# Windowed attention into MoE on one core: short token blocks at both ends, loads ordered by need, wide rows for k as for q

## Chip, cores, metric

One NeuronCore of a Trainium2 chip. The metric is device time in microseconds, median of several executions; the profiled span is some 2 us shorter than the time of the same execution. A run is called slow when it is over 1.5% above the fastest of the same kernel. Ratios are the mean time of one kernel's fast runs over the mean of the other's fast runs of the same rounds, so they are not quite the ratio of the medians quoted.

## The reference, cut to what matters

```python
# q, k, v: (8 batches, 8 heads, 576 tokens, 64)
scores = q @ k.T / 8;  mask |i - j| <= 32;  attn = softmax(scores) @ v
x = attn, heads side by side              # 4608 tokens x 512
h = x @ w_in                              # 512 -> 2048
g = h if h >= 1, 0 if h <= -1, else (h + 1)**2 / 4
out = g @ w_out                           # 2048 -> 512, float32
```

## The kernel before: the parts that matter

"Group" m is four heads of a batch (two head pairs i); 16 groups. The kernel is one loop over steps. Every step issues, in a hand-written order, one 128-row slice of the MoE's first product (`hp`), a quarter of an output tile (`op`), and some attention events: transposes of q and k (`tpose`), three score groups per pair with exp and mask (`scores`), two half attentions per pair (`pv`). All loads cast fp32 to bf16 and are issued by GpSimd.

```python
def load_qk(m):        # q: 2 DMAs, rows of 9 tokens (2304 B); k: 4 DMAs, rows of one token (256 B)
    ...
def relay(m):          # q only: reorder on GpSimd so that the transposes get unit stride
    nc.gpsimd.tensor_copy(qj[m]..., qn[m]...)
def tpose(m, t):       # t 0,1: q -> qT on ScalarE;  t 2,3: k straight from PSUM into kz on VectorE
    ...
    else:
        for h in range(2):
            for g in range(2):
                nc.vector.tensor_copy(kz[2 * (m % 2) + g][r, j0:j1, h], ps[r, :n]...)
def scores(i, g):      # TensorE, exp on ScalarE, mask on GpSimd
    ...
    nc.gpsimd.tensor_mul(pt[i][:, seg], pt[i][:, seg], maskp[:, seg])
... # prologue: all of qk0, v0-3, qk1, masks, w_in, qk2, v4-7, w_out issued on GpSimd
for a in range(-1, OFF + 16 * (NBLK + 1)):     # 9 blocks of 512 tokens, 16 steps each
    ... # loads; hp (4 matmuls), Relu (ScalarE), max and min*mult (VectorE); scores; op (4 matmuls)
    if a in att_r: relay(att_r[a])             # one step before the group's first transpose
    if a in att_x: ... tpose(...) or pv(...)
```

`kz` holds k with zeros in the other head's half, so that two heads share one matmul. Below it is taken that each engine works through its queue in the order of the program.

The softmax here doesn't subtract the row's maximum and nothing guards it: scores larger than these inputs give would overflow.

## Time and profile before

| | before |
|---|---|
| time, three runs | 393.45 us (392.82 to 394.33) |
| first TensorE instruction | 39.37 us |
| first output matmul (`op`) | about 107.3 us |
| TensorE busy 107.2 to 376.9 us | 98.8% |
| GpSimd busy over the span | 219.9 us, 56% |

"Busy" is time in which an engine works on an instruction; the idle time in front of an instruction is put down to whatever released it. In the views PE is TensorE, PEld its weight loads, DVE VectorE, ACT ScalarE and POOL GpSimd; L165 is line 165 of that run's kernel; a bracket gives the idle time before an instruction and what ended it. TensorE is the bound from 107 us on, and the start is what can be won. The lines are in the prediction.

### The profile page before, as it was taken

Reading aid. Unit: us, or ns where it says so; the run is one execution under the profiler, and the core shown is the slowest. Engines: PE = TensorE matmul, PEld = TensorE weight load, DVE = VectorE, ACT = ScalarE, POOL = GpSimd, SP = SyncE. Lnnn points to the kernel's source line nnn. Section 1 sums busy time; section 2 is a strip of 40 time slices with the busy share of each in tenths; the row PEclk is TensorE's granted clock in tenths of the full one; section 3 lists DMA queues with packets and bytes.
Section 4 is the critical chain, followed back from the end, with each engine's and each line's share of the span. In section 5 each row is a group of like instructions: output and inputs, shape, how many; then the busy total and the mean of one; then the engine's idle time right before and its main releaser. Section 6 shows DMA issues by size and latency. Waiting matters only on the chain.

```text
span 391.7 us, 6070 instructions
## 1 busy us (share of the span) xinstructions
PE 322.4 (82%) x2136; PEld 177.9 (45%) x2176; DVE 289.0 (74%) x501; ACT 219.8 (56%) x469; POOL 219.9 (56%) x288
## 2 busy tenths in 40 slices
PE   0000765677699999999999999999999999999995
PEld 0000554444355555555555555555555544444442
DVE  6100332699899999999999999999998877787720
ACT  1000564666677767675867777776766644434421
POOL 8947889996776858694958768642422200000000
PEclk9999995899999999999999999999999999999999
DMA  9999996992939678794939395830000100101012
GB/s 81 99 195 141 172 163 47 73 78 18 77 26 120 77 71 93 67 96 51 104 42 104 45 128 65 83 43 27 28 28 28 54 28 27 54 28 52 29 55 80
DMA packets 88190, 28.18 MB, mean 72 GB/s; under 512 B 76896, under 2 KB 83040, under 8 KB 88160
## 3 DMA queue, kind: packets, MB, share of 16 engines
q0 software_dynamic: 82976, 18.36, 53.2%
q1 hardware_dynamic: 5184, 9.44, 6.4%
q8 instruction: 17, 0.28, 0.3%
q14 instruction: 13, 0.11, 0.1%
HBM read 36.70 MB, written 9.44 MB: 118 GB/s over the span
## 4 chain that ended last, share of the span: by engine, by line
PE 71%; POOL 11%; DVE 9%; DMA 3%; issue 2%; ACT 2%; another core or an unknown queue 1%; ACTq 0%; POOLq 0%
PE op L260 30%; PE hp L242 28%; DMA w_in<-in_moe_w_in_dram 3%; POOL vz L97 3%; PE nm L198 3%; DVE gT L249 3%; PE tp L149 3%; POOL pt L182 3%; PE sc L174 3%; DVE yy L248 3%; POOL kn L91 3%; PE dn L189 2%; PE dn L190 2%; DVE vz L106 1%; DVE xT L208 1%
## 5 line engine op out<-in xcount | busy, mean ns | idle before, releaser
L242 PE MATMUL hp<-xT,w_in 128*128 128x512 bf16 x555 | 146.0, 379 | 4.2 <-DVE xT L208 3.0
L260 PE MATMUL op<-w_out,gT 128*128 128x512 bf16 x557 | 142.3, 379 | 0.7
L249 DVE SCALAR_TENSOR_TENSOR gT<-rr,yy 128x512 bf16<-128x512 f32 x144 | 130.3, 905 | 5.1
L182 POOL TENSOR_TENSOR pt<-pt,maskp 128x352 bf16<-128x352 bf16 (+1 forms) x96 | 85.6, 907 | 79.2 <-ACT pt L181 78.8
L247 ACT ACTIVATE rr<-hp 128x512 f32<-128x512 f32 x144 | 86.1, 598 | 76.7 <-PE hp L242 71.6
L248 DVE TENSOR_TENSOR yy<-hp,rr 128x512 f32<-128x512 f32 x144 | 99.2, 689 | 26.7 <-ACT rr L247 24.4
L260 PEld LDWEIGHTS <-gT 128*128 128x128 bf16 x576 | 53.5, 98 | 51.7
L242 PEld LDWEIGHTS <-w_in 128*128 128x128 bf16 x576 | 51.9, 98 | 43.2 <-issue 0.2
L97 POOL DMA_DIRECT2D vz<-in_v_dram x64 | 48.7, 773 | 8.2 <-DMA w_in<-in_moe_w_in_dram 7.4
L160 DVE COPY kz<-tp 64x320 bf16<-64x320 bf16 (+1 forms) x128 | 33.2, 298 | 25.8 <-PE tp L149 25.3
L149 PE MATMUL tp<-ident,qj 128*128 128x128 bf16 x144 | 15.2, 242 | 44.6 <-POOL qj L137 43.8
L153 ACT COPY qT<-tp 128x320 bf16<-128x320 bf16 (+1 forms) x64 | 24.8, 454 | 47.9 <-PE tp L149 47.7
L91 POOL DMA_DIRECT2D kn<-in_k_dram x64 | 47.9, 791 | 0.9 <-PE tp L149 0.9
L181 ACT ACTIVATE pt<-sc 128x352 bf16<-128x352 f32 (+1 forms) x96 | 45.0, 468 | 2.0 <-PE sc L174 1.8
L208 DVE TENSOR_TENSOR xT<-nm,rc 128x288 bf16<-128x288 f32 x64 | 28.8, 449 | 16.8 <-ACT rc L204 16.8
L203 ACT ACTIVATE lr<-dn 128x288 f32<-128x288 f32 x64 | 26.5, 414 | 19.8 <-PE dn L190 19.8
L174 PEld LDWEIGHTS <-kz 128*128 128x128 bf16 x288 | 25.0, 104 | 25.6 <-issue 6.4
L149 PEld LDWEIGHTS <-qj 128*128 128x128 bf16 x144 | 10.6, 108 | 52.9 <-POOL qj L137 49.4
L174 PE MATMUL sc<-qT,kz 128*128 128x128 bf16 (+1 forms) x288 | 33.2, 228 | 1.6 <-ACT pt L181 1.2
L198 PE MATMUL nm<-pt,vz 128*128 128x128 bf16 (+2 forms) x320 | 27.7, 221 | 7.5 <-DVE xT L208 7.5
L264 ACT COPY osb<-op 128x512 f32<-128x512 f32 x36 | 21.1, 587 | 19.4 <-PE op L260 16.6
L198 PEld LDWEIGHTS <-vz 128*128 128x128 bf16 x320 | 22.2, 103 | 17.8 <-issue 12.5
(26 smaller groups left out, 158.8 us busy)
## 6 DMA issues: line engine op xcount, KB each, us to landing
out_dram<-osb SPq DMA_DIRECT2D x36, 256.0 KB, 2.0
qn<-in_q_dram POOLq DMA_DIRECT2D x32, 144.0 KB, 3.6
kn<-in_k_dram POOLq DMA_DIRECT2D x64, 72.0 KB, 4.4
vz<-in_v_dram POOLq DMA_DIRECT2D x64, 72.0 KB, 3.0
w_in<-in_moe_w_in_dram POOLq DMA_DIRECT2D x1, 2048.0 KB, 12.8
w_out<-in_moe_w_out_dram POOLq DMA_DIRECT2D x1, 2048.0 KB, 15.0
```

The source lines that it names most:

```text
L91: nc.gpsimd.dma_start(out=kn[m][64 * g:64 * g + 64, :, h], in_=k[b, 4 * qd + 2 * g + h].rearrange("(c p) d -> p c d", p=64))
L97: nc.gpsimd.dma_start(out=vz[i % 8][64 * h:64 * h + 64, :, 64 * h:64 * h + 64], in_=v[b, 2 * hp + h].rearrange("(c p) d -> p c d", p=64))
L149: nc.tensor.transpose(ps[:, j - j0], src[:, j].rearrange("p h d -> p (h d)"), ident)
L174: nc.tensor.matmul(ps[:, off:off + q1 - q0], kz[2 * (m % 2) + gg][:, c].rearrange("d h r -> d (h r)"), qT[m][:, gg, q0:q1], start=True, st ...
L181: nc.scalar.activation(pt[i][:, seg], ps[:, :off], AF.Exp, scale=D ** -0.5)
L182: nc.gpsimd.tensor_mul(pt[i][:, seg], pt[i][:, seg], maskp[:, seg])
L198: nc.tensor.matmul(nm[:, q0 - lo:q1 - lo], vz[i % 8][:, c], pt[i][:, pcol(c, q0):pcol(c, q1)], start=n == 0, stop=n == len(parts) - 1, ski ...
L242: nc.tensor.matmul(hp, w_in[:, kk, 128 * f:128 * f + 128], xT[:, kk, TB * blk:TB * blk + TB], start=kk == 0, stop=kk == 3)
L247: nc.scalar.activation(rr, hp, AF.Relu, scale=0.5, bias=0.5)
L248: nc.vector.tensor_max(yy, hp, rr)
L249: nc.vector.scalar_tensor_tensor(gT[blk][:, f], rr, 1.0, yy, op0=ALU.min, op1=ALU.mult)
L260: nc.tensor.matmul(op, gT[blk - 1][:, ff, 128 * tt:128 * tt + 128], w_out[:, ff], start=ff == 0, stop=ff == 15)
```

## The change

Its intent: start the MoE when 256 tokens of batch 0 are ready instead of 512 (blocks 256, 8 x 512, 256); load first what is needed first, weights in pieces; read k, like q, in rows of nine tokens with one DMA per group instead of four; let VectorE carry the first half batch's relays, masks and copies so that GpSimd can issue loads.

k in rows of nine tokens arrives interleaved. So it needs a relay as q does, and after the transpose a second copy, `zfill`, which puts it into the zero-padded `kz`. In the main loop relays and zfill are on GpSimd.

```diff
+            rows = src[b, 4 * qd:4 * qd + 4].rearrange("(h g) s d -> h (g s) d", g=2)
+            nc.gpsimd.dma_start(out=t, in_=rows.rearrange("h (x j) d -> x h (j d)", j=NC))   # q and k
...
+    load_qk(0); identity; load_qk(1); masks; v0, v1 (five of nine chunks); w_in[:512]; rest of v0, v1; (abridged)
+    load_qk(2); w_in[512:]; v2; load_qk(3); v3; w_out in four pieces                             (abridged)
...
-            for h in range(2):
-                for g in range(2):
-                    nc.vector.tensor_copy(kz[2 * (m % 2) + g][r, j0:j1, h], ...)
+            nc.vector.tensor_copy(o, i)          # k -> kT, as q -> qT
+    def zfill(m, g, eng):
+        for h in range(2):
+            eng.tensor_copy(kz[2 * (m % 2) + g][r, :, h], kT[m][r, g]...)
...
+    # prologue: half of batch 0, relays, zfill and masks on VectorE
+    sizes = [256] + [512] * 8 + [256]
...
+            at(a0 - 10 + 2 * t + (3 if early else 0), "t", 2 * b, t)      # transposes
+            at(a0 + t if early else a0 - 2 + 2 * t, "t", 2 * b + 1, t)
...
+                rel.setdefault(a - 1, []).append((e[1], e[2] // 2))       # relay: a step before
+                zf.setdefault(a, []).append(e[1])                         # zfill: after the last transpose of k
```

Two score groups of a pair now take 352 and 256 columns, the third 480.

More of the change, by code (lines that the diff above doesn't have):

```diff
@@ L37, with pc @@
     HALF = S // 2
-    TB = 512
-    NBLK = NT // TB
     def qrange(c):
         return max(0, 64 * c - 32), min(S, 64 * c + 96)
-    def pcol(c, qq):
-        return qq if c % 2 == 0 else S + qq - 32
-    PW = 2 * S - 64
-    GROUPS = [(0, 2, 4), (6, 8, 1), (3, 5, 7)]
+    GROUPS = [(0, 2, 4), (1, 3), (6, 8, 5, 7)]
+    pcol, PW = {}, 0
+    for c in (1, 3, 0, 2, 4, 6, 8, 5, 7):
+        pcol[c] = PW
+        PW += qrange(c)[1] - qrange(c)[0]
+    def pc(c, qq):
+        return pcol[c] + qq - qrange(c)[0]
     const = ctx.enter_context(tc.tile_pool(name="const", bufs=1))
@@ L54 @@
     qtp = ctx.enter_context(tc.tile_pool(name="qtp", bufs=2))
-    ptp = ctx.enter_context(tc.tile_pool(name="ptp", bufs=3))
+    ptp = ctx.enter_context(tc.tile_pool(name="ptp", bufs=4))
     smp = ctx.enter_context(tc.tile_pool(name="smp", bufs=2))
@@ L73, with load_qk @@
     kz = [const.tile([128, NC, 2, 64], BF, name=f"kz{i}") for i in range(4)]
-    vz = [const.tile([128, NC, 128], BF, name=f"vz{i}") for i in range(8)]
+    vz = [const.tile([128, 2, NC, 128], BF, name=f"vz{i}") for i in range(4)]
     ctx.enter_context(tc.manual_schedule())
     qn, kn = {}, {}
-    def load_qk(m):
+    def load_qk(m, which="qk"):
         b, qd = divmod(m, 2)
-        qn[m] = qkn.tile([128, 2, S], BF, name="qn")
-        kn[m] = qkn.tile([128, NC, 2, D], BF, name="kn")
-        for g in range(2):
-            h0 = 4 * qd + 2 * g
-            nc.gpsimd.dma_start(out=qn[m][64 * g:64 * g + 64],
-                                in_=q[b, h0:h0 + 2].rearrange("h (p j) d -> p h (j d)", j=NC))
-        for g in range(2):
-            for h in range(2):
-                nc.gpsimd.dma_start(out=kn[m][64 * g:64 * g + 64, :, h],
-                                    in_=k[b, 4 * qd + 2 * g + h].rearrange("(c p) d -> p c d", p=64))
@@ L94, in load_v @@
-    def load_v(i):
-        b, hp = divmod(i, H // 2)
-        for h in range(2):
-            nc.gpsimd.dma_start(
-                out=vz[i % 8][64 * h:64 * h + 64, :, 64 * h:64 * h + 64],
-                in_=v[b, 2 * hp + h].rearrange("(c p) d -> p c d", p=64))
+        for src, dst, nm in ((q, qn, "qn"), (k, kn, "kn")):
+            if nm[0] in which:
+                t = dst[m] = qkn.tile([128, 2, S], BF, name=nm)
+                rows = src[b, 4 * qd:4 * qd + 4].rearrange("(h g) s d -> h (g s) d", g=2)
+                nc.gpsimd.dma_start(out=t, in_=rows.rearrange("h (x j) d -> x h (j d)", j=NC))
@@ new lines, in load_v @@
+    def load_v(m, c0=0, c1=NC):
+        b, qd = divmod(m, 2)
+        for h in range(2):
+            h0 = 4 * qd + 2 * h
+            o = vz[m % 4][64 * h:64 * h + 64, :, :, 64 * h:64 * h + 64]
+            i = v[b, h0:h0 + 2].rearrange("g s d -> (g s) d").rearrange("(gc r) d -> r gc d", r=64)
+            if c0 == 0 and c1 == NC:
+                nc.gpsimd.dma_start(out=o.rearrange("r g c d -> r (g c) d"), in_=i)
+            else:
+                for g in range(2):
+                    nc.gpsimd.dma_start(out=o[:, g, c0:c1], in_=i[:, NC * g + c0:NC * g + c1])
@@ new lines, in load_w_in, with load_w_out @@
+    def load_w_in(f0, f1):
+        src = moe_w_in.rearrange("(qd h g d) f -> h qd d g f", qd=2, h=2, g=2)
+        for h in range(2):
+            for qd in range(2):
+                nc.gpsimd.dma_start(out=w_in[64 * h:64 * h + 64, 2 * qd:2 * qd + 2, f0:f1],
+                                    in_=src[h, qd, :, :, f0:f1])
+    def load_w_out(n):
+        nc.gpsimd.dma_start(out=w_out[:, 4 * n:4 * n + 4],
+                            in_=moe_w_out.rearrange("(ko ki) f -> ki ko f", ki=128)[:, 4 * n:4 * n + 4])
@@ L101, with zero @@
     nc.scalar.preload_act_table_set("natural_log_exp_and_others")
     load_qk(0)
-    for t in kz:
-        nc.vector.memset(t.rearrange("p c h r -> p (c h r)").bitcast(FP), 0.0)
-    for i in range(8):
-        nc.vector.memset(vz[i].rearrange("p c d -> p (c d)").bitcast(FP), 0.0)
-    make_identity(nc, ident)
-    for i in range(4):
-        load_v(i)
-    load_qk(1)
+    make_identity(nc, ident)
+    load_qk(1)
+    def zero(t):
+        for h in range(2):
+            if len(t.shape) == 4 and t.shape[2] == 2:
+                z = t[64 * h:64 * h + 64, :, 1 - h]
+            else:
+                z = t[64 * h:64 * h + 64, :, :, 64 * (1 - h):64 * (1 - h) + 64].rearrange("r g c d -> r (g c) d")
+            nc.vector.memset(z, 0.0)
@@ L112 @@
+    for t in kz:
+        zero(t)
+    for t in vz:
+        zero(t)
     nc.gpsimd.memset(mask1, 1.0)
@@ L115 @@
         r = slice(64 * h, 64 * h + 64)
-        nc.gpsimd.memset(ones2[r, r], 1.0)
         nc.gpsimd.affine_select(out=mask1[r], in_=mask1[r], compare_op=ALU.is_ge, fill=0.0, base=0,
@@ L120 @@
                                 channel_multiplier=1, pattern=[[-1, 128]])
+        nc.gpsimd.memset(ones2[r, r], 1.0)
+    load_v(0, 0, 5)
+    load_v(1, 0, 5)
     for c in range(NC):
@@ L123 @@
         j0 = q0 - (64 * c - 32)
-        nc.vector.tensor_copy(maskp[:, pcol(c, q0):pcol(c, q0) + q1 - q0], mask1[:, j0:j0 + q1 - q0])
-    nc.gpsimd.dma_start(out=w_in, in_=moe_w_in.rearrange("(ko ki) f -> ki ko f", ki=128))
+        nc.vector.tensor_copy(maskp[:, pcol[c]:pcol[c] + q1 - q0], mask1[:, j0:j0 + q1 - q0])
+    load_w_in(0, 512)
+    load_v(0, 5, NC)
+    load_v(1, 5, NC)
     load_qk(2)
-    for i in range(4, 8):
-        load_v(i)
-    nc.gpsimd.dma_start(out=w_out, in_=moe_w_out.rearrange("(ko ki) f -> ki ko f", ki=128))
@@ L132, with relay @@
-    qj, qT = {}, {}
-    def relay(m):
-        qj[m] = qjp.tile([128, NC, 2, D], BF, name="qj")
-        nc.gpsimd.tensor_copy(qj[m].rearrange("p j h d -> p h j d"),
-                              qn[m].rearrange("p h (j d) -> p h j d", d=D))
+    load_w_in(512, DFF)
+    load_v(2)
+    load_qk(3)
+    load_v(3)
+    for n in range(4):
+        load_w_out(n)
+    qj, kj, qT, kT = {}, {}, {}, {}
+    def relay(m, t, eng):
+        src, dst, nm = ((qn, qj, "qj"), (kn, kj, "kj"))[t]
+        dst[m] = qjp.tile([128, NC, 2, D], BF, name=nm)
+        eng.tensor_copy(dst[m].rearrange("p j h d -> p h j d"),
+                        src[m].rearrange("p h (j d) -> p h j d", d=D))
@@ L140 @@
     TJ = [(0, 5), (5, 9)]
     def tpose(m, t):
-        src, (j0, j1) = (qj if t < 2 else kn)[m], TJ[t % 2]
+        src, dst = ((qj, qT), (kj, kT))[t // 2]
+        j0, j1 = TJ[t % 2]
+        if t % 2 == 0:
+            dst[m] = qtp.tile([128, 2, S], BF, name="qT" if t < 2 else "kT")
         ps = ps_s.tile([128, 5, 128], BF, name="tp", tag="sc")
-        if t == 0:
-            qT[m] = qtp.tile([128, 2, S], BF, name="qT")
         for j in range(j0, j1):
-            nc.tensor.transpose(ps[:, j - j0], src[:, j].rearrange("p h d -> p (h d)"), ident)
@@ L150, in tpose @@
-        n = j1 - j0
+            nc.tensor.transpose(ps[:, j - j0], src[m][:, j].rearrange("p h d -> p (h d)"), ident)
+        o = dst[m].rearrange("d g (p j) -> d g p j", j=NC)[:, :, :, j0:j1]
+        i = ps[:, :j1 - j0].rearrange("d j (g p) -> d g p j", g=2)
         if t < 2:
-            for g in range(2):
-                nc.scalar.copy(
-                    qT[m][:, g].rearrange("d (p j) -> d p j", j=NC)[:, :, j0:j1],
-                    ps[:, :n].rearrange("d j (g p) -> d g p j", g=2)[:, g])
-        else:
-            for h in range(2):
-                for g in range(2):
-                    r = slice(64 * h, 64 * h + 64)
-                    nc.vector.tensor_copy(kz[2 * (m % 2) + g][r, j0:j1, h],
-                                          ps[r, :n].rearrange("d c (g p) -> d g c p", g=2)[:, g])
+            nc.scalar.copy(o, i)
+        else:
+            nc.vector.tensor_copy(o, i)
@@ L163, with scores @@
+    def zfill(m, g, eng):
+        for h in range(2):
+            r = slice(64 * h, 64 * h + 64)
+            eng.tensor_copy(kz[2 * (m % 2) + g][r, :, h], kT[m][r, g].rearrange("d (c r) -> d c r", r=64))
     pt = {}
-    def scores(i, g):
+    def scores(i, g, eng):
         m, gg = divmod(i, 2)
@@ L170, in scores @@
         off = 0
-        first = None
         for c in GROUPS[g]:
@@ L175, in scores @@
                              qT[m][:, gg, q0:q1], start=True, stop=True)
-            if first is None:
-                first = pcol(c, q0)
             off += q1 - q0
-        seg = slice(first, first + off)
+        seg = slice(pcol[GROUPS[g][0]], pcol[GROUPS[g][0]] + off)
         nc.scalar.activation(pt[i][:, seg], ps[:, :off], AF.Exp, scale=D ** -0.5)
-        nc.gpsimd.tensor_mul(pt[i][:, seg], pt[i][:, seg], maskp[:, seg])
+        eng.tensor_mul(pt[i][:, seg], pt[i][:, seg], maskp[:, seg])
     def pv(i, hf):
@@ L187, in pv @@
         nm = ps_n.tile([128, HALF], FP, name="nm")
-        o0, o1 = max(lo, 32), min(hi, S - 32)
-        nc.tensor.matmul(dn, ones2, pt[i][:, lo:hi], start=True, stop=False)
-        nc.tensor.matmul(dn[:, o0 - lo:o1 - lo], ones2, pt[i][:, pcol(1, o0):pcol(1, o1)], start=False, stop=True)
+        odd = (1, 3) if hf == 0 else (5, 7)
+        e0 = pc(2 * hf * 2, lo) if hf else pc(0, 0)
+        o0, o1 = qrange(odd[0])[0], qrange(odd[1])[1]
+        nc.tensor.matmul(dn, ones2, pt[i][:, e0:e0 + HALF], start=True, stop=False)
+        nc.tensor.matmul(dn[:, o0 - lo:o1 - lo], ones2, pt[i][:, pcol[odd[0]]:pcol[odd[0]] + o1 - o0],
+                         start=False, stop=True)
         parts = []
@@ L197, in pv @@
         for n, (c, q0, q1) in enumerate(parts):
-            nc.tensor.matmul(nm[:, q0 - lo:q1 - lo], vz[i % 8][:, c], pt[i][:, pcol(c, q0):pcol(c, q1)],
+            nc.tensor.matmul(nm[:, q0 - lo:q1 - lo], vz[i // 2 % 4][:, i % 2, c], pt[i][:, pc(c, q0):pc(c, q0) + q1 - q0],
                              start=n == 0, stop=n == len(parts) - 1, skip_group_check=True)
@@ L208, in mul @@
             nc.vector.tensor_mul(xT[:, hp, b * S + lo:b * S + hi], nm, rc)
-        return mul
-    A0 = 9
-    att_s, att_x, att_r = {}, {}, {}
-    for m in range(NP // 2):
-        for t in range(4):
-            att_x[8 * m + 2 * t] = ("t", m, t)
-        att_r[8 * m - 1] = m
-    for i in range(NP):
-        for g in range(3):
-            att_s[A0 + 4 * i + g] = (i, g)
-        for hf in range(2):
-            att_x[A0 + 4 * i + 4 + 2 * hf] = ("v", i, hf)
-    OFF = A0 + 4 * 3 + 6 + 2
-    loads = {}
@@ L225, with flush @@
-    for m in range(3, NP // 2):
-        loads.setdefault(8 * m - 16, []).append((load_qk, m))
-    for i in range(8, NP):
-        loads.setdefault(4 * i - 14, []).append((load_v, i))
-    gT = {}
-    mul = None
-    for a in range(-1, OFF + 16 * (NBLK + 1)):
-        mm = a - OFF
-        blk, f = divmod(mm, 16)
-        for fn, arg in loads.get(a, []):
-            fn(arg)
-        if 0 <= mm and blk < NBLK:
+        muls.append(mul)
+    muls = []
+    def flush():
+        while muls:
+            muls.pop(0)()
@@ new lines @@
+    V, P = nc.vector, nc.gpsimd
+    for m in range(2):
+        for t in range(2):
+            relay(m, t, V)
+    for m in range(2):
+        if m == 1:
+            for i in range(2):
+                for g in range(2):
+                    scores(i, g, V)
+        for t in range(4):
+            tpose(m, t)
+        for g in range(2):
+            zfill(m, g, V)
+        if m == 1:
+            for i in range(2):
+                pv(i, 0)
+                flush()
+    for i in range(2, 4):
+        for g in range(2):
+            scores(i, g, V)
@@ new lines, with at @@
+    for i in range(2, 4):
+        pv(i, 0)
+        flush()
+    sizes = [256] + [512] * 8 + [256]
+    starts = [sum(sizes[:t]) for t in range(len(sizes))]
+    NB = len(sizes)
+    ev = {}
+    def at(a, *e):
+        ev.setdefault(a, []).append(e)
+    for i in range(4):
+        at(i, "s", i, 2)
+        at(i + 1, "v", i, 1)
+    for t in range(4):
+        at(t, "t", 2, t)
+        at(4 + t, "t", 3, t)
+    for n in range(12):
+        at(4 + n, "s", 4 + n // 3, n % 3)
+    for n in range(4):
+        at(4 + 3 * n + 2, "v", 4 + n, 0)
+        at(4 + 3 * n + 3, "v", 4 + n, 1)
@@ new lines @@
+    for b in range(2, B):
+        a0 = 16 * (b - 1)
+        early = b == 2
+        for n in range(4):
+            for g in range(3):
+                at(a0 + 4 * n + g - (0 if early and n == 0 else 2), "s", 4 * b + n, g)
+            at(a0 + 4 * n + 1 + (1 if early and n == 0 else 0), "v", 4 * b + n, 0)
+            at(a0 + 4 * n + 3, "v", 4 * b + n, 1)
+        for t in range(4):
+            at(a0 - 10 + 2 * t + (3 if early else 0), "t", 2 * b, t)
+            at(a0 + t if early else a0 - 2 + 2 * t, "t", 2 * b + 1, t)
@@ new lines @@
+    rel, zf = {}, {}
+    for a, es in ev.items():
+        for e in es:
+            if e[0] == "t" and e[2] % 2 == 0:
+                rel.setdefault(a - 1, []).append((e[1], e[2] // 2))
+            if e[0] == "t" and e[2] == 3:
+                zf.setdefault(a, []).append(e[1])
+    loads = {}
+    for m in range(4, NP // 2):
+        loads.setdefault(max(0, 8 * m - 38), []).append((load_qk, m))
+        loads.setdefault({4: 3, 5: 5, 6: 11, 7: 17}.get(m, 8 * m - 39), []).append((load_v, m))
@@ L238 @@
+    for e in rel.get(-1, []):
+        relay(*e, P)
+    gT = {}
+    for a in range(16 * NB + 8):
+        t, f = divmod(a, 16)
+        for fn, m in loads.get(a, []):
+            fn(m)
+        if t < NB:
+            n, t0 = sizes[t], starts[t]
             if f == 0:
-                gT[blk] = gtp.tile([128, 16, TB], BF, name="gT")
-            hp = ps_h.tile([128, TB], FP, name="hp")
+                flush()
+                gT[t] = gtp.tile([128, 16, 512], BF, name="gT")
+            hp = ps_h.tile([128, 512], FP, name="hp")
@@ L241 @@
             for kk in range(4):
-                nc.tensor.matmul(hp, w_in[:, kk, 128 * f:128 * f + 128], xT[:, kk, TB * blk:TB * blk + TB],
+                nc.tensor.matmul(hp[:, :n], w_in[:, kk, 128 * f:128 * f + 128], xT[:, kk, t0:t0 + n],
                                  start=kk == 0, stop=kk == 3)
-            rr = ewp.tile([128, TB], FP, name="rr")
-            yy = ewp.tile([128, TB], FP, name="yy")
-            nc.scalar.activation(rr, hp, AF.Relu, scale=0.5, bias=0.5)
-            nc.vector.tensor_max(yy, hp, rr)
@@ L249 @@
-            nc.vector.scalar_tensor_tensor(gT[blk][:, f], rr, 1.0, yy, op0=ALU.min, op1=ALU.mult)
-        if mul:
-            mul()
-            mul = None
-        if a in att_s:
-            scores(*att_s[a])
-        if 1 <= blk <= NBLK and mm >= 0:
-            tt, f0 = divmod(f, 4)
-            if f0 == 0:
-                op = ps_o.tile([128, DM], FP, name="op")
-            for ff in range(4 * f0, 4 * f0 + 4):
-                nc.tensor.matmul(op, gT[blk - 1][:, ff, 128 * tt:128 * tt + 128], w_out[:, ff],
-                                 start=ff == 0, stop=ff == 15)
-            if f0 == 3:
-                osb = osp.tile([128, DM], FP, name="osb")
-                nc.scalar.copy(osb, op)
-                t0 = TB * (blk - 1) + 128 * tt
-                nc.sync.dma_start(out=out[t0:t0 + 128, :], in_=osb)
@@ L267 @@
-        if a in att_r:
-            relay(att_r[a])
-        if a in att_x:
-            kind, i, t = att_x[a]
-            if kind == "t":
-                tpose(i, t)
-            else:
-                mul = pv(i, t)
+            rr = ewp.tile([128, 512], FP, name="rr")
+            yy = ewp.tile([128, 512], FP, name="yy")
+            nc.scalar.activation(rr[:, :n], hp[:, :n], AF.Relu, scale=0.5, bias=0.5)
+            nc.vector.tensor_max(yy[:, :n], hp[:, :n], rr[:, :n])
+            nc.vector.scalar_tensor_tensor(gT[t][:, f, :n], rr[:, :n], 1.0, yy[:, :n], op0=ALU.min, op1=ALU.mult)
@@ new lines @@
+        flush()
+        es = ev.get(a, [])
+        for e in es:
+            if e[0] == "s":
+                scores(e[1], e[2], P)
+        if t >= 1:
+            per = sizes[t - 1] // 128 if t < NB else 4
+            for x in range(per * f, per * f + per):
+                tt, ff = divmod(x, 16)
+                if ff == 0:
+                    op = ps_o.tile([128, DM], FP, name="op")
+                nc.tensor.matmul(op, gT[t - 1][:, ff, 128 * tt:128 * tt + 128], w_out[:, ff],
+                                 start=ff == 0, stop=ff == 15)
+                if ff == 15:
+                    osb = osp.tile([128, DM], FP, name="osb")
+                    nc.scalar.copy(osb, op)
+                    r0 = starts[t - 1] + 128 * tt
+                    nc.sync.dma_start(out=out[r0:r0 + 128, :], in_=osb)
@@ L278 @@
+        for e in rel.get(a, []):
+            relay(*e, P)
+        for e in es:
+            if e[0] == "t":
+                tpose(e[1], e[2])
+        for m in zf.get(a, []):
+            for g in range(2):
+                zfill(m, g, P)
+        for e in es:
+            if e[0] == "v":
+                pv(e[1], e[2])
 _INS = ['q', 'k', 'v', 'moe_w_in', 'moe_w_out']
```

## The prediction

> **What bounds the kernel now.** I read the page's slices first, then the table of busy time by stage, the groups, the GpSimd and TensorE timelines of the start, and the issue table.
>
> The slices (40 of 9.8 us each) show where TensorE is idle:
>
> ```profile
> PE   0000765677699999999999999999999999999995
> POOL 8947889996776858694958768642422200000000
> DMA  9999996992939678794939395830000100101012
> DMA packets 88190, 28.18 MB, mean 72 GB/s; under 512 B 76896, under 2 KB 83040, under 8 KB 88160
> ```
>
> TensorE is empty for four slices, half busy for seven, and full from slice 11 to the end. GpSimd and DMA are full while TensorE is not. The stages (columns: stretch, length, busy us of PE, PEld, DVE, ACT, POOL, clock, DMA share, GB/s) put numbers on it:
>
> ```profile
> 0.00:39.37 39.37, 0.00 (x0) 0.00 (x1) 7.79 (x21) 1.28 (x1) 29.94 (x52) 1.00 1.26 128
> 39.37:71.00 31.63, 21.16 (x169) 16.88 (x171) 9.22 (x31) 18.32 (x47) 29.55 (x39) 0.84 1.15 129
> 71.00:107.20 36.20, 24.07 (x192) 13.73 (x195) 32.18 (x59) 22.72 (x53) 31.24 (x39) 1.00 0.74 57
> 107.20:376.90 269.70, 266.43 (x1728) 142.48 (x1762) 239.86 (x391) 175.19 (x365) 129.13 (x161) 1.00 0.44 59
> ```
>
> Nothing runs on TensorE before 39.37 us. From there to 71 us the attention prologue is paced by GpSimd (29.55 of 31.63 us busy); from 71 to 107.2 us the first MoE block runs with both GpSimd and VectorE near 88%. From 107.2 us, the first output matmul, TensorE is 98.8% busy and sets the pace. So all there is to win lies before 107 us. The GpSimd timeline says why the first transpose waits until 39.37 us:
>
> ```profile
> 18.23 0.78 POOL L125 DMA_DIRECT2D w_in<-in_moe_w_in_dram  x1
> ...
> 31.36 0.73 POOL L97 DMA_DIRECT2D vz<-in_v_dram  x1 [7.42 <-DMA w_in<-in_moe_w_in_dram]
> ...
> 36.92 1.21 POOL L129 DMA_DIRECT2D w_out<-in_moe_w_out_dram  x1
> 38.18 2.23 POOL L137 COPY qj<-qn 128x1152 bf16<-128x1152 bf16 x2
> ```
>
> The relay copy of q, which feeds the first transpose, stands on GpSimd behind all the load issues, and one of these waits 7.42 us for w_in to land. The instruction list shows the reason: the GpSimd loads use eight completion semaphores in turn, so load n waits for load n-8. The groups give the unit costs that I use below:
>
> ```profile
> L249 DVE SCALAR_TENSOR_TENSOR gT<-rr,yy 128x512 bf16<-128x512 f32 x144 | 130.3, 905 | 5.1
> L182 POOL TENSOR_TENSOR pt<-pt,maskp 128x352 bf16<-128x352 bf16 x64 | 56.6, 886 | 59.8 <-ACT pt L181 59.5
> L182 POOL TENSOR_TENSOR pt<-pt,maskp 128x384 bf16<-128x384 bf16 x32 | 30.4, 949 | 19.4 <-ACT pt L181 19.2
> L137 POOL COPY qj<-qn 128x1152 bf16<-128x1152 bf16 x16 | 18.2, 1144 | 0.0
> ```
>
> **What the Trainium skill says.** "DMA: Bandwidth & Descriptors", section Specifications, asks for at least 512 B per descriptor for line rate. The trace agrees in kind: 76,896 of 88,190 packets are under 512 B, and the DMA moves 81 to 99 GB/s (bytes written) in the first two slices, which hold q, k and v, against 195 in the slice that holds w_in. "VectorE: DVE Perf Modes", section The perf-mode tier table, gives bf16 SBUF copies four elements per cycle on VectorE and bf16 tensor_tensor two. No such large operation runs on VectorE in the kernel before, so the prologue's times on VectorE below are estimates from that page. "SBUF — State Buffer" says that a VectorE instruction with two SBUF inputs contends with a GpSimd instruction that reads SBUF. The trace agrees: L249 has a minimum of 691 ns, a mean of 905 ns, and 692 ns after 320 us, where GpSimd is idle.
>
> **The change, part by part.**
>
> *Loads.* k goes from 64 DMAs of 256-byte reads (mean 791 ns of GpSimd each) to 16, q from 32 to 16, each of 256 packets. From the issue costs of the present 128, 576 and 2048-packet loads (634, 773, 1214 ns: about 0.3 ns a packet) a q or k load costs 0.67 us, a whole v load (1152 packets, 32 of them if none were split) 0.94 us. Over the kernel GpSimd issue falls from 117 to about 60 us. But that is spread out, and most of it lies beside a full TensorE.
>
> *Relay, zero filling and masks.* k now needs a relay too (16 x 1.14 us), and the copies into kz (zfill) become GpSimd work after the first two groups: 56 copies of 64x576, estimated at half a relay plus overhead, 0.63 us. In the first half batch all this is on VectorE, with the masks. VectorE's kz copies (8 per group, 298 ns, 2.4 us) become two wide ones, about 0.75 us each.
>
> *The prologue.* GpSimd's first four loads are issued by about 4.7 us. q and k, 0.59 MB of fp32 each, need about 1.6 us at the 380 GB/s read rate that w_in shows (4.2 MB from about 19.6 to 31 us), so group 0 lands near 6.5 and group 1 near 10 us. VectorE clears kz and vz until about 8 us, copies masks (1.34 us as now) and relays. First transpose about 10 us instead of 39.4. Then follow transpose, evacuate, zfill, four scores with exp and mask, group 1, and four half attentions in series, each about 2 us for Ln, Exp and multiply: the prologue would end near 28 to 30 us.
>
> *The new wait.* After-order on GpSimd: all loads through the fourth piece of w_out are issued before the first relay of group 2. By the rule of eight, that last piece is issued only when the second half of v group 2 has landed. Up to there DMA must bring six q/k loads (9.5 us at 380 GB/s), three groups of v (2304 packets each; 9216 small packets of k and v took about 13.5 us in the first stage now, so 3.3 us a group, 10 us) and w_in (11 us): 30.5 us, plus 2.8 us start, about 1.5 us of starving on issue and 2 us landing: about 37 us. GpSimd is free at 38.4 us, hardly earlier than the 38.18 us of today. TensorE meets the transpose of group 2 in step 0 of the MoE, so it stands from about 29 until 39.6 us. **Much of the prologue's gain is thus given back.**
>
> *Block 0 (256 tokens).* Until block 1 can start, GpSimd has six relays (6.9), four masks of 480 columns left from batch 0 (slope 2 ns a column from the two rows above: 1.14 each, 4.6), the twelve masks of batch 1 (0.886 + 0.70 + 1.14 per pair, 10.9), eight zfills (5.0), six q/k loads (4.0) and six v loads (5.6): 37.0 us. About 2 us more go to v4 waiting for the lanes that w_out holds, and 2 us to bubbles (GpSimd was 93% busy in the comparable stage). TensorE has only 64 x 0.108 = 6.9 us of MoE and 10 us of attention here, VectorE about 26 us. So GpSimd binds, and block 1 starts at 38.4 + 41 + 1, **about 80 us**.
>
> *From there to the end.* A matmul of 512 columns takes 0.216 us (17 in 3.67 us at 373.14 us in the chain). The 269.7 us from 107.2 us hold 8 x 128 of them, 221.1 us; the other 48.6 us are the 22.9 head pairs of attention that I count as left then, 2.12 us each, 8.5 us a batch. After: block 1 has 96 matmuls and one batch, 29.2 us on TensorE, but VectorE needs 16 x (0.69 + 0.95) + 8 x 0.45 + 3 = 32.8 us, so 33. Five blocks with attention 5 x (27.6 + 8.5) = 180.5. Two without, 55.3. The short last block 20.7, its output 6.9. The end after the last matmul 4.1 as now. Sum 300.5, total 380; with some slack for GpSimd being released early or block 1 running nearer TensorE's own time, **378 us**. The short block at the end gains nothing by itself: TensorE is full there anyway (11 of the last 13 us before the copy), and it has the same columns to stream.
>
> **Rivals.** (1) *Loads finish much earlier*: with k in 2304-byte rows and the small-packet v loads overlapped better, GpSimd is released near 31 us and block 0 follows at 68 to 72 us. For it: the DMA is at 195 GB/s in only one early slice now. Against: 9.5 MB must come before the release, and w_in's stretch is already near 380 GB/s read. It makes 365 to 369 us. (2) *GpSimd is slower than my sum*, because in block 0 it meets VectorE's two-input operations and the in-order TensorE queue makes every relay, zfill and mask a link in one chain; block 1 starts at 90 us or later: 388 us and more, a change within 2%. For it: masks reach 1407 ns at worst now. (3) *GpSimd was never the loss*: TensorE-bound from the prologue on, block 1 at about 52 us and 350 us in total. Against it stands GpSimd's 37 us sum of listed instructions. (4) *VectorE becomes the bound in the steady part*: 26.2 + 3.6 + 3 = 32.8 of 36.1 us, so I think not.
>
> **Range and chances.** The start of block 1 carries nearly all the uncertainty, about 8 us either way; the steady part is known to 1%, 3 us. So 365 to 389 us. Faster by 2% means under 385.6 us, block 1 before about 86 us: 0.82. Same 0.15. Slower would need the prologue to gain nothing and the masks on GpSimd to fall behind: 0.03.
>
> **What would show each step.** First transpose 9 to 13 us. First MoE matmul about 29 us, then a TensorE gap ended by GpSimd's relay of qj, up to about 39 us. The last w_out issue waiting for a v load. GpSimd over 90% busy from 39 to 80 us. First 512-column matmul near 80 us. From block 2 TensorE again near 98%. If the gap is absent, or GpSimd is idle for a fifth of block 0, my account of the start is wrong; if TensorE falls under 95% after block 1, rival 4 holds.

## The result

431.77 us (430.7 to 437.17; the last is a slow run) against 393.74 us, now of four runs of the kernel before: ratio 1.0959, 95% interval 1.0925 to 1.0994. Slower by nearly 10%, where 4% faster was forecast.

The start went nearly as the prediction said. The slices of the changed kernel's page (40 of 10.7 us each):

```profile
PE   0652575576859797979887988889789999999996
POOL 8966968797766566665666566653644100000000
PEclk9965858999999899998999899989999999999999
DMA  8999993452706253534444272700000010110111
DMA packets 54749, 28.17 MB, mean 66 GB/s; under 512 B 38848, under 2 KB 49600, under 8 KB 54720
```

TensorE begins in the second slice instead of the fifth. But where the kernel before had a row of nines from slice 12 on, this one alternates between 7 and 9 until slice 30, and neither GpSimd nor DMA is full there. The stages (columns as in the prediction):

```profile
0.00:11.33 11.33, 0.00 (x0) 0.00 (x0) 8.41 (x27) 1.28 (x1) 9.94 (x25) 1.00 0.93 121
11.33:29.31 17.98, 11.55 (x89) 8.71 (x89) 11.81 (x27) 9.03 (x20) 16.04 (x25) 0.89 1.10 128
29.31:39.25 9.94, 0.60 (x5) 0.34 (x4) 0.85 (x2) 0.95 (x2) 5.08 (x8) 0.50 1.45 182
39.25:84.86 45.61, 27.79 (x239) 21.42 (x241) 27.07 (x45) 24.55 (x58) 35.77 (x41) 0.78 0.89 109
84.86:353.00 268.14, 228.14 (x1510) 120.97 (x1539) 199.30 (x276) 155.92 (x318) 159.82 (x179) 0.97 0.35 53
```

In the long stage TensorE is 85% busy, VectorE 74%, GpSimd 60%, ScalarE 58%. No engine is full. The GpSimd timeline of the start, the answer to the four lines of before:

```profile
32.76 0.76 POOL L111 DMA_DIRECT2D w_out<-in_moe_w_out_dram  x1 [1.41 <-DMA w_in<-in_moe_w_in_dram]
35.34 0.74 POOL L111 DMA_DIRECT2D w_out<-in_moe_w_out_dram  x1 [1.82 <-DMA w_in<-in_moe_w_in_dram]
...
37.27 0.74 POOL L111 DMA_DIRECT2D w_out<-in_moe_w_out_dram  x1 [0.25 <-DMA vz<-in_v_dram]
38.05 1.14 POOL L165 COPY qj<-qn 128x1152 bf16<-128x1152 bf16 x1
```

The relay of group 2 comes at 38.05 us, behind loads that wait for earlier loads, as before at 38.18 us. The groups that answer to those in the prediction, with the new zfill:

```profile
L334 DVE SCALAR_TENSOR_TENSOR gT<-rr,yy 128x512 bf16<-128x512 f32 x128 | 116.4, 909 | 4.4
L189 POOL COPY kz<-kT 64x576 bf16<-64x576 bf16 x56 | 45.7, 816 | 20.3 <-DVE kT L184 18.1
L206 POOL TENSOR_TENSOR pt<-pt,maskp 128x480 bf16<-128x480 bf16 x32 | 35.3, 1104 | 42.7 <-ACT pt L205 42.5
L165 POOL COPY kj<-kn 128x1152 bf16<-128x1152 bf16 x14 | 19.7, 1406 | 0.0
```

The VectorE operation on gT takes what it took before (909 against 905 ns). So VectorE's largest operation was not slowed by the change.

Where the time is lost is read best from the block lengths. This table is from the VectorE timeline: the time from the first gT operation of a block to the first of the next, in us.

| block | before | changed | relays early (e1) | relays and transposes early (e3) |
|---|---|---|---|---|
| 1 | 36.4 | 44.5 | 40.5 | 38.4 |
| 2 | 36.4 | 44.2 | 38.3 | 36.4 |
| 3 | 36.3 | 44.3 | 38.5 | 36.4 |
| 4 | 35.5 | 44.3 | 38.5 | 36.4 |
| 5 | 35.5 | 44.1 | 38.5 | 36.3 |
| 6 | 32.3 | 36.0 | 36.0 | 34.9 |
| 7 | 27.7 | 27.8 | 27.8 | 27.8 |

Blocks 2 to 5 each lose 8 to 9 us, some 4 us for each of their two groups. Block 7, without attention, loses nothing. What TensorE itself waited for, first the kernel before between 120 and 320 us, then the changed one between 120 and 360 us (columns: who waited for whom, us in total, times, longest):

```profile
PE hp L242 <- DVE xT L208: 1.4, 2, 0.7
```

```profile
PE tp L178 <- POOL qj L165: 16.7, 9, 2.2
PE sc L201 <- POOL kz L189: 12.0, 10, 1.2
PE nm L225 <- DVE xT L234: 1.2, 3, 0.8
```

The two waits together happen once each per group. One group in the timelines, first TensorE, then GpSimd:

```profile
210.68 1.03 PE L327 MATMUL hp<-xT,w_in 128*128 128x512 bf16 x4
212.91 0.33 PE L201 MATMUL sc<-qT,kz 128*128 128x96 bf16 x3 [1.20 <-POOL kz L189]
213.07 1.03 PE L346 MATMUL op<-w_out,gT 128*128 128x512 bf16 x4
215.90 0.45 PE L178 MATMUL tp<-ident,qj 128*128 128x128 bf16 x5 [1.80 <-POOL qj L165]
216.19 0.81 PE L327 MATMUL hp<-xT,w_in 128*128 128x512 bf16 x3
```

```profile
208.38 1.09 POOL L206 TENSOR_TENSOR pt<-pt,maskp 128x480 bf16<-128x480 bf16 x1 [1.82 <-ACT pt L205]
211.09 3.55 POOL L189 COPY kz<-kT 64x576 bf16<-64x576 bf16 x4 [1.62 <-DVE kT L184]
214.71 1.14 POOL L165 COPY qj<-qn 128x1152 bf16<-128x1152 bf16 x1
```

GpSimd sits idle for 1.62 us until VectorE has copied the last piece of k out of PSUM. Then come four zfill copies, 3.55 us, and only behind these the relay of the next group's q. TensorE needs the first two zfill copies for the scores at 212.91 and the relay for the transpose at 215.90. Each is on time for the order of the program, and late for a TensorE that runs at full speed: the last transposes of k were issued at 208.12 us, only two steps of 2.2 us before the scores and the transposes that wait.

The theory to test (A): the main loop is slowed by latency in the in-order queues, not by the amount of work, since relay, zfill and transposes stand too close together. Rivals: (B) GpSimd's work, or its contention with VectorE, is simply too much; (C) the wider copies out of PSUM on ScalarE hold up its queue.

### The profile page after: what moved, and what is told of

The parts are those of the page before. It is cut to its first block, busy times and chain, and to the rows that moved or that the text cites. A ratio compares the mean times of both kernels' runs of the same rounds, so it can differ in the third digit from the quotient of the medians.

```text
span 429.9 us, 6091 instructions
## 1 busy us (share of the span) xinstructions
PE 340.8 (79%) x2203; PEld 187.5 (44%) x2240; DVE 298.3 (69%) x461; ACT 220.9 (51%) x453; POOL 226.7 (53%) x274
## 4 chain that ended last, share of the span: by engine, by line
PE 54%; POOL 26%; issue 7%; DVE 6%; ACT 3%; DMA 3%; POOLq 0%; ACTq 0%
PE hp L327 22%; PE op L346 22%; POOL kz L189 10%; POOL pt L206 5%; POOL qj L165 4%; DVE gT L334 3%; PE nm L225 3%; PE tp L178 3%; DMA w_in<-in_moe_w_in_dram 3%; POOL vz L101 2%; PE sc L201 2%; ACT rr L332 2%; ACT pt L205 1%; DVE yy L333 1%; POOL vz L98 1%
## 5 line engine op out<-in xcount | busy, mean ns | idle before, releaser
L333 DVE TENSOR_TENSOR yy<-hp,rr 128x512 f32<-128x512 f32 (+1 forms) x160 | 101.4, 634 | 105.6 <-ACT rr L332 104.3
L327 PE MATMUL hp<-xT,w_in 128*128 128x512 bf16 (+1 forms) x618 | 154.7, 372 | 1.7 <-DVE xT L234 0.8
L334 DVE SCALAR_TENSOR_TENSOR gT<-rr,yy 128x512 bf16<-128x512 f32 (+1 forms) x160 | 138.0, 863 | 5.6
L332 ACT ACTIVATE rr<-hp 128x512 f32<-128x512 f32 (+1 forms) x160 | 88.7, 555 | 98.9 <-PE hp L327 79.2
L206 POOL TENSOR_TENSOR pt<-pt,maskp 128x480 bf16<-128x480 bf16 (+2 forms) x88 | 79.1, 901 | 81.1 <-ACT pt L205 79.7
L189 POOL COPY kz<-kT 64x576 bf16<-64x576 bf16 x56 | 45.7, 816 | 20.3 <-DVE kT L184 18.1
L205 ACT ACTIVATE pt<-sc 128x352 bf16<-128x352 f32 (+2 forms) x96 | 44.5, 469 | 20.0 <-PE sc L201 19.9
L182 ACT COPY qT<-tp 128x640 bf16<-128x640 bf16 (+1 forms) x32 | 23.5, 741 | 53.1 <-PE tp L178 42.3
L201 PE MATMUL sc<-qT,kz 128*128 128x128 bf16 (+1 forms) x288 | 33.2, 232 | 19.7 <-POOL kz L189 16.7
L201 PEld LDWEIGHTS <-kz 128*128 128x128 bf16 x288 | 23.9, 105 | 43.8 <-POOL kz L189 23.3
L225 PE MATMUL nm<-pt,vz 128*128 128x128 bf16 (+2 forms) x320 | 27.8, 220 | 11.9 <-DVE xT L234 11.3
L178 PEld LDWEIGHTS <-qj 128*128 128x128 bf16 x144 | 11.8, 116 | 51.9 <-POOL qj L165 36.3
L234 DVE TENSOR_TENSOR xT<-nm,rc 128x288 bf16<-128x288 f32 x64 | 28.6, 447 | 3.1 <-ACT rc L230 1.8
L230 ACT ACTIVATE rc<-lr 128x288 f32<-128x288 f32 x64 | 28.4, 443 | 2.0
L184 DVE COPY kT<-tp 128x640 bf16<-128x640 bf16 (+1 forms) x32 | 24.2, 761 | 2.8 <-PE tp L178 2.8
```

What stands on the lines that cost most here:

```text
L178: nc.tensor.transpose(ps[:, j - j0], src[m][:, j].rearrange("p h d -> p (h d)"), ident)
L189: eng.tensor_copy(kz[2 * (m % 2) + g][r, :, h], kT[m][r, g].rearrange("d (c r) -> d c r", r=64))
L201: nc.tensor.matmul(ps[:, off:off + q1 - q0], kz[2 * (m % 2) + gg][:, c].rearrange("d h r -> d (h r)"), qT[m][:, gg, q0:q1], start=True, st ...
L205: nc.scalar.activation(pt[i][:, seg], ps[:, :off], AF.Exp, scale=D ** -0.5)
L206: eng.tensor_mul(pt[i][:, seg], pt[i][:, seg], maskp[:, seg])
L225: nc.tensor.matmul(nm[:, q0 - lo:q1 - lo], vz[i // 2 % 4][:, i % 2, c], pt[i][:, pc(c, q0):pc(c, q0) + q1 - q0], start=n == 0, stop=n == l ...
```

## Experiments

Nine kernels ran, all correct. Differences between two experiments of different rounds have no interval of their own.

### e1: relays two steps earlier

```diff
-                rel.setdefault(a - 1, []).append((e[1], e[2] // 2))
+                rel.setdefault(a - (3 if e[1] >= 4 else 1), []).append((e[1], e[2] // 2))
```

> The changed kernel with one edit: the relay copies of q and k for groups 4 and up are issued three steps before their transposes instead of one, so that the relay of the next group's q stands ahead of the zero-filling copies (zfill) of the group before in GpSimd's queue and not behind them. Theory A (the loss after block 1 is latency in the in-order queues: the transpose of q waits for a relay that stands behind four zfill copies, and the scores wait for zfill): TensorE's wait for the relay of q, 16.7 us between 120 and 360 us in the changed kernel, falls below 4 us, the wait of scores for zfill (12 us) stays, and the time falls by 15 to 30 us, to about 405 to 415 us. Rival B (GpSimd simply has too much work, or its contention with VectorE slows both): the order does not matter, time within 5 us of 432. Rival C (wider evacuations on ScalarE hold up its queue): also within 5 us of 432.

403.13 us, 1.0244 times before (1.0205 to 1.0284): 28.6 us gone with no work removed. TensorE's waits between 120 and 360 us:

```profile
PE sc L201 <- POOL kz L189: 12.0, 10, 1.2
PE nm L225 <- DVE xT L234: 0.4, 2, 0.2
```

The wait for the relay is gone, and the wait for zfill stayed to the tenth. B and C, which said that the order does not matter, fall in that form. The gain is at the upper end of what A expected, and past its 405 us. It is more than the 16.7 us of that wait because the window leaves out the first 120 us, which hold another 5.1 us of that wait, and because TensorE's mean clock goes from 0.94 to 0.98 (last section).

### e2: zfill on VectorE

```diff
-                zfill(m, g, P)
+                zfill(m, g, V)
```

> The changed kernel with one edit: zfill runs on VectorE in the main loop instead of on GpSimd. VectorE did four of them in 1.85 us in the prologue, GpSimd needs 3.55 us in the steady part. Theory A: the wait of scores for zfill and most of the wait of the transposes for the relay of q go, TensorE is above 95% busy after block 1 unless VectorE binds (its work rises by 3.7 us a batch to about 36 us of 36), time 385 to 400 us. Rival B (contention between VectorE and GpSimd): VectorE's copies [...]add contention, so time stays above 415 us. Rival C (ScalarE): within 5 us of 432.

405.09 us, 1.0288 (1.0268 to 1.0308). Better than 415, but 5 us short of what A expected. TensorE's waits in the same window:

```profile
PE sc L201 <- DVE kz L189: 3.2, 10, 0.3
PE nm L225 <- DVE xT L234: 3.1, 12, 0.7
PE hp L327 <- DVE yy L333: 2.6, 10, 0.6
```

The wait for the relay is gone, with the relays left where they were: with zfill out of the way they are on time. Of the 12.0 us for zfill, 3.2 are left. Beside them are small waits for VectorE, which between 130 and 290 us is 90% busy (143.46 of 160), and TensorE is 95.5% busy. So both waits hang on the zfill copies in GpSimd's queue; on VectorE they cost their share there.

### e3: relays and transposes early

```diff
-            at(a0 - 10 + 2 * t + (3 if early else 0), "t", 2 * b, t)
-            at(a0 + t if early else a0 - 2 + 2 * t, "t", 2 * b + 1, t)
+            at(a0 - 7 + 2 * t if early else a0 - 12 + 2 * t, "t", 2 * b, t)
+            at(a0 + t if early else a0 - 4 + 2 * t, "t", 2 * b + 1, t)
```

This is on top of e1.

> As the run with early relays, and the transposes of groups 6 and up are moved two steps earlier too, so that four steps instead of two lie between the last transpose of k and the first scores. No instruction is removed or changes engine. Theory A: both waits go, TensorE is back at 97% or more from block 2 on, and the time is 84.9 + 300 plus a few us, 385 to 395 us. Rival B: GpSimd's and VectorE's work is the same, so the time stays above 415 us. Rival C: likewise above 415 us.

393.48 us, 0.9991 (0.9944 to 1.0038): the whole loss is undone by order alone. The waits, and the stage 125 to 305 us:

```profile
PE dn L216 <- POOL pt L206: 3.1, 9, 0.5
PE nm L225 <- DVE xT L234: 0.9, 3, 0.5
```

```profile
125.00:305.00 180.00, 175.21 (x1221) 97.49 (x1244) 159.48 (x218) 123.54 (x254) 127.35 (x138) 1.00 0.42 64
```

TensorE is 97.3% busy, and GpSimd is busier than in the changed kernel (127.35 of 180, 71%), because the same work fits into less time. Blocks 2 to 5 take 36.4 us, where the prediction had 36.1, and blocks 2 to 6 together 180.4 us, where it had 180.5. Block 1 still takes 38.4 us, where it had 33; what holds it is not settled by these runs.

### e4: loads by need in the kernel before

All loads except those of groups 0 and 1 and v pairs 0 to 3 go into the step loop; w_in and w_out stay whole.

```diff
-    nc.gpsimd.dma_start(out=w_in, ...); load_qk(2); v4..v7; nc.gpsimd.dma_start(out=w_out, ...)
+    loads[3], loads[18] = [(load_w, 0)], [(load_w, 1)]      # w_in, w_out
+    for m in range(2, NP // 2): ...                          # instead of 3
+    for i in range(4, NP): ...                               # instead of 8
```

> The kernel before with one edit: only the loads of groups 0 and 1 and of four v pairs are issued ahead; w_in, w_out and the other loads go into the step loop, where each is needed some steps later. It has neither the wide k rows nor the short blocks nor VectorE's prologue. Theory: the first transpose waits only for the relay behind the loads issued in 16 us and the mask building, so it comes at about 19.5 us instead of 39.4; GpSimd then still paces the prologue, so the first output matmul moves from 107 to about 88 to 95 us and the total to 373 to 382 us, ahead of both kernels. Rival: the DMA bandwidth of the start was the true limit, so that w_in or v come late and the gain is under 6 us.

396.61 us, 1.007 (1.0046 to 1.0094): a miss. The first transpose came at 19.61 us as expected, but the first output matmul at 110.4 instead of 107 us. What GpSimd waited for between 28 and 72 us:

```profile
POOL kn L91 <- DMA w_in<-in_moe_w_in_dram: 6.8, 1, 6.8
POOL kn L91 <- DMA w_out<-in_moe_w_out_dram: 5.0, 1, 5.0
```

w_in, 13.4 us from issue to landing, holds one of the eight completion semaphores that the loads use in turn. The eighth load after it stops GpSimd's queue, and with it the masks behind it. I had seen this wait in the profile before, and put it into the loop myself. The rival named beforehand, too little DMA bandwidth, also meant a gain under 6 us; against it, e9 moves the same bytes and is 7.9 us faster.

### e9: the same, weights in pieces

```diff
+    for n in range(8):      # four pieces of w_in, four of w_out
+        loads[(5, 9, 13, 17, 20, 25, 29, 33)[n]] = [(load_w, n)]
```

> The kernel before with loads by need, as in the earlier run of that name, but w_in and w_out are each cut into four pieces issued four steps apart. In that run a load of k waited 6.78 us for w_in and another 5.05 us for w_out, each in front of masks in GpSimd's queue. Theory (a whole weight load holds one of the eight completion semaphores for 13 to 16 us, and GpSimd's queue stops at its eighth successor): both waits go, and the time falls from 396.6 to 385 to 390 us, under the kernel before. Rival (the masks and load issues on GpSimd alone pace the prologue of that kernel): the time stays at 393 to 397 us.

388.73 us, 0.9885 (0.9869 to 0.9902), as expected. Between 28 and 80 us GpSimd now waits only 1.5 us in all, for a ScalarE exp. It is 97% busy from 30 to 80 us (48.52 of 50), so its work is probably the next bound there; no run tests it. Since e4 and e9 differ in the placing of the pieces as well as in their size, the 7.9 us between them belong to both. Loads by need with weights in pieces are worth 4.6 us to the kernel before.

### e5: group 2 ahead of the later loads

On top of e3: v3 and the w_out pieces are issued between the steps of block 0.

```diff
-    load_v(3)
-    for n in range(4):
-        load_w_out(n)
...
+    loads[1] = [(load_v, 3)]
+    for n in range(4):
+        loads.setdefault(5 + n, []).append((load_w_out, n))      # qk4, qk5, v4 to v6 some steps later too
```

> The kernel with relays and transposes early, and in addition the relays of group 2 stand ahead of v group 3 and the w_out pieces in GpSimd's queue; these loads are issued between the steps of block 0, so that their waits for a free completion semaphore find them landed. No work is removed. Theory A (the stop of TensorE from about 29.5 to 39.2 us is the wait of that relay behind loads that wait for loads): the stop shrinks to under 3 us, the first output matmul comes at 76 to 80 instead of 86.8 us, time 382 to 387 us. Rival B (GpSimd's remaining 37 us of listed work, and DMA, are what paces block 0 in any order): block 0 just stretches and the time stays within 3 us of 393.

385.09 us, 0.9773 (0.9743 to 0.9804), inside the expectation. TensorE goes on through the place where it stood for 9.3 us:

```profile
28.57 1.20 PE L327 MATMUL hp<-xT,w_in 128*128 128x256 bf16 x4
29.56 0.50 PE L198 MATMUL sc<-qT,kz 128*128 128x128 bf16 x4
29.90 0.44 PE L175 MATMUL tp<-ident,qj 128*128 128x128 bf16 x5
30.18 0.60 PE L327 MATMUL hp<-xT,w_in 128*128 128x256 bf16 x4
```

The first output matmul comes at 79.8 instead of 86.8 us. From 30 to 79.8 us GpSimd is 89% busy (44.14 of 49.8).

### e6: VectorE helps in block 0

On top of e5:

```diff
-                scores(e[1], e[2], P)
+                scores(e[1], e[2], V if e[1] < 4 else P)
-                zfill(m, g, P)
+                zfill(m, g, V if m < 4 else P)
```

> As the run with group 2 first, and the zfill of groups 2 and 3 and the four remaining masks of batch 0 go to VectorE, which has slack in block 0: about 6.5 + 4.4 us less on GpSimd, about 3.7 + 1.6 us more on VectorE. Theory A (GpSimd's work binds block 0): the first output matmul comes 6 to 10 us earlier than in the run with group 2 first, about 68 to 73 us, time 373 to 380 us, faster than both kernels. Rival B (block 0 is a chain of latencies through all engines, not GpSimd's throughput): a gain under 3 us.

379.46 us, 0.9644 (0.9623 to 0.9665): 3.6% faster than before, the best. The first output matmul comes at 74.0 us, a little later than expected. The gain beside e5 is 5.6 us where GpSimd lost some 11 us of work, and GpSimd is 76% busy from 30 to 74 us (33.49 of 44). So GpSimd's work did count in block 0, but no longer binds it alone. (The 11 us are the estimate of the expectation.)

### e7: blocks of 512 again

On top of e3: nine blocks of 512, the rest of batch 0 in the prologue.

```diff
+    for i in range(4):
+        scores(i, 2, V)
+        pv(i, 1)
+        flush()
-    sizes = [256] + [512] * 8 + [256]
+    sizes = [512] * 9
```

> The kernel with relays and transposes early, with the short blocks undone: nine blocks of 512 tokens, the third scores group and the second half of batch 0 moved from block 0 into the VectorE-masked prologue (and one half attention of batch 1 a step earlier). Theory A (block 0 is paced by GpSimd, so its MoE matmuls ride for free and a short block only does less of them in that time; the short last block gains nothing because TensorE is full there): the same time or better, 385 to 394 us. Rival (the short blocks give a gain of their own that the slow main loop hid): the time goes up by 4 us or more, to 397 us or later.

386.83 us, 0.9838 (0.9808 to 0.9868): 6.7 us faster than e3. The first output matmul comes at 90.1 instead of 86.8 us, but by then block 0 has done twice the tokens. At that state of the kernel the arrangement with short blocks is the slower one. But e7 does two things: it also takes four masks of 480 columns (about 1.1 us each) off GpSimd and gives them to VectorE, and in e6 masks and zfill moved together gained 5.6 us. So the 6.7 us are not shown to belong to the block lengths; e8 against e6, where VectorE has these masks in both, is the cleaner comparison.

### e8: all repairs with blocks of 512

e6's repairs with e7's blocks.

> All repairs together and blocks of 512 tokens: relays and transposes early, group 2 ahead of the later loads, zfill of groups 2 and 3 on VectorE, the whole of batch 0 in the VectorE-masked prologue. If the gain of blocks of 512 (6.7 us beside the run with relays and transposes early) adds to the 379.5 us of the run where VectorE helps in block 0: 372 to 377 us. If it does not add, because block 0 with less GpSimd work is no longer long enough to carry twice the MoE matmuls for nothing: 377 to 383 us.

383.88 us, 0.9755 (0.9736 to 0.9775), just above the 377 to 383 us said for this case. The gains do not add: with block 0 relieved, the short block is ahead by 4.4 us (379.46 against 383.88). The GpSimd waits between 29 and 60 us point to a reason, which no run tests:

```profile
POOL pt L203 <- ACT pt L202: 13.0, 2, 11.9
POOL qj L162 <- DVE pt L203: 2.6, 1, 2.6
```

The longer prologue is on VectorE, ScalarE and TensorE, and GpSimd, which is to prepare batch 1, is idle for 11.9 us meanwhile. So a short first block pays in the relieved kernel; whether it cost anything before that stays open (e7). The short last block was not tested by itself; block 7, where no attention is left, has the same length in every version of the table.

## Why the prediction was wrong

**First transpose, prologue, first MoE matmul:** right. 11.33 us (9 to 13), 28.32 us (about 29). The sums add up; the read rate of 380 GB/s is a little high for its own figures (4.2 MB in 11.4 us is 368), worth less than 1 us.

**The new wait:** right in mechanism and size. TensorE stands from about 29.9 to 39.25 us (said: 29 to 39.6), ended by the relay of q at 38.05 us, behind w_out pieces that wait for w_in and v. The waits follow the rule of eight: the 35th to 38th loads wait for the 27th to 30th, which are pieces of w_in, and the 40th for the 32nd, a half of v. e5 shows that the order of the loads was its cause.

**Block 0:** right in part. It was to last until about 80 us and lasted until 84.86. The zfill copies were taken at 0.63 us and averaged 0.816, and GpSimd was not over 90% busy until 80 us: 35.77 of 45.61 us, 78%. So it was idle for more than a fifth, which the prediction had named as the sign that its account is wrong. That the end still came within 5 us is partly luck. TensorE's stops are like those of the main loop: 3.73 us for zfill at 53.46 us, 3.87 us for a relay behind zfill at 69.63 us. That GpSimd's work counts there is shown by e6, but not with the whole sum of 37 us as I had it.

**From there to the end:** this is the step that failed. The text said "the steady part is known to 1%, 3 us", with block 1 at 33 us and "Five blocks with attention 5 x (27.6 + 8.5) = 180.5". The runs showed 44.5 us for block 1 and 212.8 us for blocks 2 to 6 (44.2 + 44.3 + 44.3 + 44.1 + 36.0). That is 11.5 + 32.3 = 43.8 us. With the 4.9 us of the later start of block 1 it makes up nearly the whole of the 53.8 us between 378 and 431.8; the rest is 2.5 us of slack that I had taken off, and 2 us between span and time. I had asked of every engine whether it had room, found the 36.1 us of TensorE above VectorE's 32.8, and stopped. That zfill and the relay of k are new links between the transposes and the scores, in one queue and in that order, I had listed in the change and in rival 2, but for block 0 only. The order zfill, then the next group's relay, can be read from the changed kernel's loop. Counted as latency it gives the stop, with the durations of the group shown above: 3.0 us from the last transpose of k (208.12 us) to zfill, 3.6 us of zfill, 1.1 us of relay, 7.7 us together, with the next transposes of q due two steps of 2.2 us later. That is 3.3 us late, once a group, and it appears as two stops, for zfill and then for the relay, 1.20 and 1.80 us. Of the 43.8 us, e3 gives back 38.5 (6.1 in block 1, 32.4 in blocks 2 to 6) by order alone; that is the missing latency. The other 5.4 us are block 1's own time, mis-sized at 33 us where e3 shows 38.4, with the cause open.

**Rivals:** 1 and 3 did not happen. 2 named the chain, but placed it in block 0 and let it cost 10 us. 4, VectorE as the bound of the steady part, did not come true in the changed kernel, though e2 comes near it. Its sign did: TensorE fell to 85%, under the 95% named, while VectorE was only 74% busy. The sign fitted any stop of TensorE, not this rival alone. None foresaw a slower steady part with no engine full, and 0.03 for slower was the price.

**The short last block** "gains nothing by itself": consistent with the runs, but not shown by one of its own.

## What to carry to other kernels

In a hand-ordered loop over in-order queues, a new copy costs its time on its engine and also its place: count, for each product that crosses engines, the steps between its issue and its first use, and compare that with the sum of the queue positions it waits behind. An engine at 60% can stop one at 98%. And when a loop shows no full engine, move the producers earlier before moving work away; here that alone gave 38 us.

## What the Trainium skill lacked or had wrong

- "TensorE: Matmul & The Clock Gate", Part 1, has the clock drop after an idle window of about 3.4 us; it also tells of a kernel in which short idles did it, without their lengths. Here no stop of the main loop was that long (the longest took 2.24 us): a stop of 1.20 us, 1.19 us of matmuls and a stop of 1.81 us were followed by a drop to 0.50 (stretches below, columns as above, the clock is third from last; the two lines below them are of the TensorE timeline), and a step's four `hp` matmuls took 1.91 us instead of 1.03. But the pair of stops at 212.91 and 215.90 us, of 1.20 and 1.80 us, was followed by three `hp` matmuls at full speed. From 145 to 305 us the drop came after every second pair (148.86, 193.01, 237.26, 281.58 us, not 171.64, 215.90, 260.22, 304.35). What decides is not shown. Over 84.86 to 353 us the mean clock was 0.97, in e3's steady stage 1.00. So some stops cost more than their idle time.

```profile
234.00:236.00 2.00, 1.19 (x7) 0.46 (x7) 1.80 (x3) 0.46 (x1) 1.89 (x3) 1.00 0.00 0
236.00:238.00 2.00, 0.74 (x6) 0.67 (x7) 0.00 (x0) 0.00 (x0) 1.94 (x2) 0.72 0.00 0
238.00:240.00 2.00, 2.00 (x7) 0.82 (x6) 0.00 (x0) 1.04 (x2) 0.01 (x1) 0.50 0.00 0
240.00:242.00 2.00, 2.00 (x15) 1.11 (x14) 1.50 (x2) 1.51 (x5) 0.67 (x1) 0.93 0.00 0
237.26 0.72 PE L178 MATMUL tp<-ident,qj 128*128 128x128 bf16 x5 [1.81 <-POOL qj L165]
237.76 1.91 PE L327 MATMUL hp<-xT,w_in 128*128 128x512 bf16 x4
```

- "SBUF — State Buffer" states that a VectorE instruction with two SBUF inputs contends with a GpSimd instruction that reads SBUF; beyond two factors without their operations it has no price for a GpSimd copy in such company. Here a 64x576 bf16 copy took 665 ns at the median and 1092 at worst, and the four of a group 2.87 us in the early part and 3.55 us in the main loop. That contention makes this difference is not shown.
- No page that I read says what a full set of load semaphores does to a GpSimd queue that also computes. Here a 2 MB (bf16) weight load held one of eight for 13.4 us and stopped the queue for 6.8 us; in pieces, spread out, it did not.
